# First projection in two token halves, one block's statistics on ScalarE, a shorter root, and where weight work is placed

## The chip, the cores and the metric

The kernel runs on one core of one Trainium2 chip. The metric is device microseconds (us) of one execution; before the change three runs gave 808.19, 809.09 and 808.35 us, median 808.35. Engines are called PE (TensorE, matmuls), PEld (its weight loads), DVE (VectorE), ACT (ScalarE), POOL (GpSimd) and SP (SyncE, which here issues nearly all DMAs). Each engine runs its own list of instructions strictly in the order of the list.

## What is computed

Layer norm of `x` (2048 tokens of 512), then a sliding-window attention with 32 heads of 16 and a window of 256, and beside it a SwiGLU block of width 1792; the output is `x + attention * silu(swiglu)`.

```
xn = _layernorm(x)                                   # (x - mean) / sqrt(var + 1e-5), no affine
qkv = (xn @ wqkv) -> q, k, v                         # 32 heads of 16
scores = q . k * 16**-0.5, masked to 0 <= i - j < 256
s = softmax(scores) @ v, heads joined, @ wo
h = silu(xn @ w1) * (xn @ w3)                        # 512 -> 1792
g = silu(h @ w2)                                     # 1792 -> 512
out = x + s * g
```

## The kernel before

**Precision.** Each operand of a dense matmul is cut into two 16-bit parts, a high and a low one, and a product is made as three matmuls: high·high, low weight·high token, high weight·low token. Weights are first scaled by a power of two that comes from the sum of squares of the rows. So a weight block passes through these steps: a DMA load in f32; its squares summed (`squares`, on ACT at L249 or on DVE at L251); the sums cast to bf16 (`cast`, L261, DVE) and summed over partitions by a one-column matmul (`powers`, L280); the scale made of them on DVE (L291, L298, L302, L304); and the cut into high and low. The cut is `split` (high on ACT, L333; low on DVE, L334) or `split_pool` (scaling and high on ACT, L342 and L343; low on POOL in four pieces, L345).

**Stages.** Tokens go in four tiles of 512 (`t` = 0 to 3). `prepare(t)` loads four blocks of 128 tokens, takes mean and variance of each (`stats`: L438 and L439, on DVE), the reciprocal root for all four at once (`rstd`), subtracts and multiplies (`centre`, L477) and turns each block on PE (`turn`, L493); ACT copies the turned block as the high part `XH` (L496), DVE makes the low part `XL` (L501). `project(t, g, k)` then makes queries (`k` = 0) or keys (`k` = 1) of eight heads (L597), stored through ACT (L614) and DVE (L618) to DRAM and fetched from there in the layout of the heads (`fetch`, L643). `value` makes the values (L567). In the steady part each of 32 units (`t`, `g`, `p`) runs a first pass for the row maxima (`pass1`, scores at L667, maxima on DVE at L681) for a later unit, and a second pass (`pass2`: scores at L748, mask added on DVE at L755, exponential on ACT at L758, values at L776), with pieces of the SwiGLU between them (`gate_up`, L1048, tanh on ACT at L1063, products on DVE at L1067 and L1072, a copy at L1081; `down`, L1273). The weights of the SwiGLU are loaded and prepared during the first tile (`measure`, `measure_down`): `measure` handles two blocks of `w1` and `w3`, four squares of 512 columns.

**The order of the work.** PE's list is the order in which the program is written. The lists of DVE, ACT, POOL and SP are set by a planner at build time; `urgent()` raises an instruction's priority in it, and `tc.issue_after(ins)` keeps the instructions inside from being planned before `ins`. That is a matter of the plan alone: the order of an engine's list comes out of it, no wait on the chip. `lasts` holds such anchors: `lasts["exp"]` is the exponential issued last (L758), `behind_exp()` puts work behind it, and `lasts["emptied"]` is the DVE instruction that last freed a PSUM bank. `later(n, f)` runs `f` after `n` further pieces of PE's work.

**The start** (the part that the change rewrites). ACT fills `KA[1]` with ones (L1525). DVE takes the statistics of all four blocks. The root is a shift, a subtraction (L447, L448) and then a cubic and a Newton step (L451 to L459); the Newton step is kept behind the cast of the first weight sums. The centring stands behind the scale of the first weights. Matmuls of ones (`keep_busy`, L1549) fill PE while it has nothing: 24 at first, 3 ahead of the turning and 3 behind it. Then follow on PE: keys of head group 0 with the high tokens (`k00[0]`, four matmuls of 512 columns), queries likewise (`q00[0]`), the low weights of the keys (`k00[1]`), a one-column sum for the next weights (L280), the low weights of the queries (`q00[1]`), the low tokens of both, and the keys of group 1 (`k01`).

## Time and profile before

| | |
|---|---|
| median of three runs | 808.35 us |
| the profiled execution | 808.19 us, of which 806.4 us are its span (first to last instruction) and 1.79 us lie around it |
| busy, share of the span | PE 98%, DVE 78%, ACT 49%, POOL 47% |
| TensorE clock granted | full in all 40 slices |
| DMA queue of SP and ACT | 132.13 MB, 55.9% of 16 engines' span |

All times below are of that one execution, in us from the span's start. In a row of the timeline the first number is the start, the second the length, then engine, line, operation, out<-in with shapes, how many instructions are merged, and in brackets how long the engine stood idle before it and what released it. A matmul's length includes its way through the array; in a stream the next one starts long before it ends (216 ns after it for 512 columns, 109 ns for 256), so the share of busy time says little about PE, and its idle gaps a lot. In the chain of waits the profile goes back from the last instruction, at each step to what released it.

### The profile page before, as it was taken

To read this page: it belongs to the slowest core of one execution; us is meant where nothing else is said; L and a number is where in the kernel's file an instruction comes from. 1 tells how busy PE (TensorE), PEld (TensorE's weight loads), DVE (VectorE), ACT (ScalarE), POOL (GpSimd) and SP (SyncE) were. 2 spreads that over 40 slices of the span, in tenths; PEclk is the share of its full clock that TensorE was granted. 3 is DMA by queue.
4 is the path that set the end of the run, shared out by engine and by line. 5 is a ranking of instruction groups with operands and counts; after the bars stand their busy time and mean duration, and the time that the engine had idled before them with its cause. 6 is when DMAs were issued, how large, how long until landed. Compare 5 with 4: busy or idle time off the path is not lost.

```text
span 806.4 us, 23975 instructions
## 1 busy us (share of the span) xinstructions
PE 792.3 (98%) x9175; PEld 403.6 (50%) x9175; DVE 630.9 (78%) x2037; ACT 392.5 (49%) x591; POOL 377.5 (47%) x732
## 2 busy tenths in 40 slices
PE   8999999999999999999999999999999999999997
PEld 4444444444544444444445444466544754466465
DVE  8888888798898778887888888777768886875537
ACT  6878686663456535345443443434444234344411
POOL 2345357352439345355352555430346276650670
PEclk9999999999999999999999999999999999999999
DMA  9887554746666574658456733656462654334431
GB/s 282 241 259 241 176 177 121 260 121 196 189 194 197 151 241 129 220 150 268 118 180 177 216 110 94 187 150 186 133 169 84 160 135 132 87 89 158 129 93 59
DMA packets 109859, 134.19 MB, mean 166 GB/s; under 512 B 18928, under 2 KB 64944, under 8 KB 109744
## 3 DMA queue, kind: packets, MB, share of 16 engines
q1 hardware_dynamic: 109456, 132.13, 55.9%
q8 instruction: 72, 1.18, 0.6%
q10 hardware_dynamic: 288, 0.52, 0.2%
q14 instruction: 43, 0.35, 0.1%
HBM read 91.23 MB, written 36.57 MB: 158 GB/s over the span
## 4 chain that ended last, share of the span: by engine, by line
PE 83%; DVE 6%; ACT 6%; DMA 2%; issue 2%; SPq 1%; POOL 0%; DVEq 0%; ACTq 0%
PE m L1048 30%; PE po L776 9%; PE m L1273 9%; PE m L597 8%; PE m L1191 8%; PE s L748 5%; PE m L1325 4%; PE m L567 4%; PE s L667 3%; PE po L667 2%; ACT pt L758 1%; DVE junk L681 1%; ACT slot L342 1%; DMA slot<-in_B_w_dram 1%; ACT slot L343 1%
## 5 line engine op out<-in xcount | busy, mean ns | idle before, releaser
L1048 PE MATMUL m<-XH,slot 128*128 128x512 f16 x896 | 267.3, 380 | 1.3 <-DVE slot L618 0.8
L758 ACT ACTIVATE pt<-s,es 128x1024 f32<-128x1024 f32 x152 | 167.6, 1113 | 190.9 <-DVE s L755 179.2
L1048 PEld LDWEIGHTS <-slot 128*128 128x128 f16 x1344 | 124.9, 98 | 155.2 <-issue 11.5
L1048 PE MATMUL m<-XL,slot 128*128 128x512 f16 x448 | 169.8, 379 | 0.0
L755 DVE TENSOR_TENSOR s<-s,MK 128x256 f32<-128x256 f32 (+2 forms) x280 | 118.8, 435 | 51.9 <-PE s L748 48.9
L681 DVE CUSTOM_DVE_ANT_0 junk<-s,MW 128x320 bf16<-128x320 f32 x276 | 134.1, 486 | 17.6 <-PE s L667 9.8
L339 POOL TENSOR_TENSOR slot<-slot,slot 128x256 f16<-128x256 f32 (+1 forms) x86 | 57.6, 692 | 126.8 <-ACT slot L1081 56.7
L345 POOL TENSOR_TENSOR slot<-slot,slot 128x128 f16<-128x128 f32 x168 | 68.8, 445 | 69.7 <-ACT slot L343 67.7
L681 DVE CUSTOM_DVE_ANT_0 junk<-po,MW 128x320 bf16<-128x320 f32 x172 | 83.5, 485 | 4.7 <-DVE al L298 0.4
L1273 PE MATMUL m<-slot,slot 128*128 128x512 f16 x336 | 78.6, 380 | 0.1
L776 PE MATMUL po<-pt,V 64*32 64x320 f32 (+4 forms) x2880 | 77.2, 342 | 1.5 <-DVE pp L304 1.5
L597 PE MATMUL m<-XH,slot 128*128 128x512 f16 x240 | 70.9, 380 | 1.1 <-DVE slot L1067 0.7
L1191 PE MATMUL m<-slot,slot 128*128 128x256 f16 x588 | 68.4, 273 | 0.0
L1106 POOL TENSOR_TENSOR slot<-slot,slot 128x256 f16<-128x256 f32 x98 | 64.6, 672 | 1.1
L1063 ACT ACTIVATE slot<-m,sgs 128x512 f32<-128x512 f32 x56 | 38.3, 683 | 54.0 <-PE m L1048 53.8
L776 PEld LDWEIGHTS po<-pt,V 64*32 64x32 f32 x2880 | 50.4, 106 | 23.6 <-issue 2.4
L1191 PEld LDWEIGHTS <-slot 128*128 128x128 f16 x588 | 56.2, 98 | 11.4 <-issue 2.8
L1067 DVE SCALAR_TENSOR_TENSOR slot<-slot,m 128x512 f32<-128x512 f32 x56 | 38.3, 685 | 28.6 <-ACT slot L1063 27.1
L748 PE MATMUL s<-qa,KA 50*64 50x320 f16 (+3 forms) x1472 | 58.3, 259 | 0.2 <-DVE M L681 0.2
L597 PEld LDWEIGHTS <-slot 128*128 128x128 f16 x384 | 35.6, 98 | 44.6 <-issue 3.1
L748 PEld LDWEIGHTS <-KA 50*64 50x64 f16 x1472 | 30.1, 105 | 52.0 <-issue 31.4
L1273 PEld LDWEIGHTS <-slot 128*128 128x128 f16 x336 | 30.7, 98 | 38.4 <-issue 4.0
(190 smaller groups left out, 1138.8 us busy)
## 6 DMA issues: line engine op xcount, KB each, us to landing
slot<-dW SPq DMA_DIRECT2D x98, 256.0 KB
slot<-in_B_w_dram SPq DMA_DIRECT2D x56, 256.0 KB
slot<-dFold SPq DMA_DIRECT2D x48, 256.0 KB
dW<-slot SPq DMA_DIRECT2D x42, 256.0 KB
slot<-in_A_x_dram SPq DMA_DIRECT2D x30, 256.0 KB
KA<-dK SPq DMA_DIRECT2D x24, 288.0 KB
slot<-dWQ SPq DMA_DIRECT2D x24, 256.0 KB
qa<-dQ SPq DMA_DIRECT2D x30, 192.0 KB
```

What stands on the lines that cost most here:

```text
L339: op(out[:, c], a[:, c], b[:, c])
L345: nc.gpsimd.tensor_sub(lo[:, c:c + P], raw[:, c:c + P], hi[:, c:c + P])
L597: nc.tensor.matmul(cell["pp"], w[:, (a * NC + c) * P:(a * NC + c + 1) * P], b[:, c, :], start=(c, i) == parts[0][0], stop=(c, i) == parts[ ...
L681: lasts["maximum"] = nc.vector.tensor_tensor_reduce(out=junk[:, :n], in0=s[:, r, :n], in1=mask, scale=1.0, scalar=NEG, op0=ALU.add, op1=AL ...
L748: nc.tensor.matmul(s[64 * h:64 * h + 64, r, o:o + 64 * n], ka[rows, 2 * p + a, 64 * (m + 4):64 * (m + 5)], qa[rows, 2 * p + a, 64 * (m + k ...
L755: nc.vector.tensor_add(v, v, MK[:, kind, of:of + n, :].unsqueeze(1).to_broadcast([P, 2 * len(which), n, 64]))
L758: lasts["exp"] = nc.scalar.activation(pt, s, AF.Exp, scale=es)
L776: nc.tensor.matmul(cell["po"][32 * i:32 * i + 32, h, 64 * (m + k):64 * (m + k + n)], V[64 * h:64 * h + 64, (4 * t + m // 2) % VB, hd * VW: ...
L1048: nc.tensor.matmul(cell[k], w[:, (a * NC + c) * P:(a * NC + c + 1) * P], b[:, c, :], start=c == 0 and i == 0, stop=c == NC - 1 and i == 2)
L1106: nc.gpsimd.tensor_sub(lo, view, hi)
L1191: nc.tensor.matmul(cell["ps"][:, c], made[:, f:f + P], wj[:, g:g + 256], start=j == j0 and c == 0 and n == 0, stop=j == j1 - 1 and n == 2, ...
L1273: nc.tensor.matmul(ps, hh[:, a * TW + b * P:a * TW + (b + 1) * P], w[:, c * D:(c + 1) * D], start=f == f0 and i == 0, stop=f == f1 - 1 and ...
```

## The change

- `stats` of block 3 of the first tile goes to ACT: a copy with accumulation (the sum), a one-element step that makes minus the mean, a square with that as bias and accumulation (the variance); DVE only scales both sums by 1/512. For that ACT's fill of `KA[1]` goes to POOL.
- `rstd` of the first tile stays at nine operations on DVE behind `ve`. Before, each needed the one ahead of it; now two of them (both on `r0`) stand beside the chain, which is seven deep, and the hold behind the cast is gone.
- `project` can run its first part in two halves of 256 columns (tokens 0 to 255, then 256 to 511): `k00` begins with high and low weights for the first half, then for the second, then the queries. The three matmuls of ones ahead of it go.
- The squares that `measure` puts on ACT later on are planned behind `lasts["exp"]`, which is now also set by the projections' copy (L614) and by tanh (L1063). So the planner's lists for ACT, DVE, POOL and SP differ up to about 270 us of the program.

```diff
@@ squares
+        def behind(i, raw):
+            with behind_exp() if i < on_act and "emptied" in lasts else nullcontext():
+                one(i, raw)
         for i, raw in enumerate(parts):
             if apart:
-                later(apart * (i + 1), lambda i=i, raw=raw: one(i, raw))
+                later(apart * (i + 1), lambda i=i, raw=raw: behind(i, raw))
@@ prepare: stats
+            if t == 0 and b == 3:
...
+                nc.scalar.activation(junk, xts[b], AF.Copy, accum_out=acc[:, 0:1])
+                nc.scalar.activation(neg, acc[:, 0:1], AF.Copy, scale=-1.0 / D)
...
+                nc.scalar.activation(junk, xts[b], AF.Square, bias=neg, accum_out=acc[:, 1:2])
+                nc.vector.tensor_scalar(mv[:, b, :], acc, 1.0 / D, None, op0=ALU.mult)
+                return
@@ prepare: rstd
+            if t == 0:
...
+                nc.vector.tensor_scalar(r0.bitcast(I32), ve.bitcast(I32), -0.5, float(0x5F3759DF), op0=ALU.mult, op1=ALU.add)
+                nc.vector.tensor_mul(sq, r0, r0)
+                nc.vector.tensor_mul(y, sq, ve)
+                nc.vector.tensor_scalar(r0, r0, -0.5 * (9 / 64) * (3 / 8) * XS, None, op0=ALU.mult)
+                nc.vector.scalar_tensor_tensor(sq, y, -10 / 3, y, op0=ALU.add, op1=ALU.mult)
+                nc.vector.scalar_tensor_tensor(z, sq, 5.0, y, op0=ALU.add, op1=ALU.mult)
+                nc.vector.scalar_tensor_tensor(r0, sq, 5.0, r0, op0=ALU.add, op1=ALU.mult)
+                nc.vector.scalar_tensor_tensor(z, sq, 5.0, z, op0=ALU.add, op1=ALU.mult)
+                nc.vector.scalar_tensor_tensor(rs[:, b0:b1], z, -64 / 3, r0, op0=ALU.add, op1=ALU.mult)
+                return
...
-                nc.vector.scalar_tensor_tensor(r0, sq, 5.0, r0, op0=ALU.add, op1=ALU.mult)
-                with tc.issue_after(lasts["cast"].ins):
-                    nc.vector.tensor_mul(sq, r0, r0)
-                nc.vector.scalar_tensor_tensor(sq, sq, -0.5 * (3 / 8)**3 * XS, ve, op0=ALU.mult, op1=ALU.mult)
-                nc.vector.scalar_tensor_tensor(rs[:, b0:b1], sq, 1.5 * (3 / 8) * XS, r0, op0=ALU.add, op1=ALU.mult)
-                return
@@ project
+        cols = [slice(0, TW)] * len(parts)
+        if halved:
+            parts.insert(0, parts[0])
+            cols = [slice(0, TW // 2), slice(TW // 2, TW)] + cols[1:]
...
-                nc.scalar.activation(B[:, 0, :], pp, AF.Copy, scale=s)
+                lasts["exp"] = nc.scalar.activation(B[:, 0, :], pp, AF.Copy, scale=s)
@@ gate_up
-                    nc.scalar.activation(sg, cell[0], AF.Tanh, scale=sg_scale[:, f:f + 1])
+                    lasts["exp"] = nc.scalar.activation(sg, cell[0], AF.Tanh, scale=sg_scale[:, f:f + 1])
@@ the start
-    nc.scalar.activation(KA[1].rearrange("p a (b c) -> p (a b) c", c=P), onesb.unsqueeze(1).to_broadcast([P, 24, P]),
-                         AF.Copy, scale=ONE)
...
-    for a in range(4):
-        nc.gpsimd.memset(KA[2][:, a, :].bitcast(F32), TWO_ONES)
+    for ka in KA[1:]:
+        for a in range(4):
+            nc.gpsimd.memset(ka[:, a, :].bitcast(F32), TWO_ONES)
...
-    keep_busy(3, waiting[:, 0, :].rearrange("p (k q) -> p k q", q=P))
-    k00, q00 = (project(0, 0, k, ((0,), (1,), (2,)), (lambda: waiting) if k else False) for k in (1, 0))
-    run([k00[0], q00[0], k00[1]])
+    k00 = project(0, 0, 1, ((0, 1), (2,)), lambda: waiting, True)
+    q00 = project(0, 0, 0, ((0,), (1,), (2,)))
+    run(k00[:2] + q00[:2])
     qk[1][2]()
...
-    run([q00[1]])
```

How the lists stand at the three places that the prediction speaks of. Line numbers of the changed kernel run ahead of those of the kernel before: its L444, L445 and L447 are the new ACT steps, L448 DVE's scaling, L451 and L452 the statistics, L456 to L473 the root, L249 the squares, L264 the cast, L283, L294, L301 and L305 the scale, L336 and L337 the cut, L345 and L346 `split_pool`'s ACT steps, L778 the exponential, L1083 tanh, L951 the squares for `w2`.

The first place is the start on ACT and on DVE. ACT before:

```order
L1525 ACT_TABLE_LOAD
L1525 ACTIVATE KA_141<-onesb 128x3072
L249 ACTIVATE sqa,ssq<-slot_177 128x512
L249 ACTIVATE sqa,ssq<-slot_178 128x512
L333 ACTIVATE slot_307<-slot_178,sw_277 128x512
```

and with the change:

```order
L444 ACT_TABLE_LOAD
L444 ACTIVATE sqa,acc<-slot_173 128x512
L445 ACTIVATE neg<-acc 128x1
L447 ACTIVATE sqa,acc<-slot_173,neg 128x512
L249 ACTIVATE sqa,ssq<-slot_176 128x512
L249 ACTIVATE sqa,ssq<-slot_177 128x512
L336 ACTIVATE slot_317<-slot_177,sw_285 128x512
```

The two squares of the first weights (L249) now stand behind the statistics of block 3. DVE before, from the last steps of the root (`sb` is the cast of the weight sums, `rs` the root's result, `sw` the scale):

```order
L455 SCALAR_TENSOR_TENSOR r_292<-sq,r_292 128x4
L261 CAST sb<-ssq 128x2
L457 TENSOR_TENSOR sq<-r_292 128x4
L458 SCALAR_TENSOR_TENSOR sq<-sq,ve 128x4
L291 TENSOR_SCALAR al<-s 128x1
L459 SCALAR_TENSOR_TENSOR rs<-sq,r_292 128x4
L298 TENSOR_SCALAR al<-al 128x1
L302 TENSOR_SCALAR sw_277<-al 128x1
```

and with the change:

```order
L469 SCALAR_TENSOR_TENSOR sq<-y 128x4
L470 SCALAR_TENSOR_TENSOR z<-sq,y 128x4
L471 SCALAR_TENSOR_TENSOR r_300<-sq,r_300 128x4
L472 TENSOR_TENSOR z<-sq,z 128x4
L473 SCALAR_TENSOR_TENSOR rs<-z,r_300 128x4
L264 CAST sb<-ssq 128x2
L294 TENSOR_SCALAR al<-s 128x1
L301 TENSOR_SCALAR al<-al 128x1
L305 TENSOR_SCALAR sw_285<-al 128x1
```

The cast stood in the middle of the root; it now stands behind the whole of it.

The second place is SP's list at about 22 to 36 us: the stores of keys and queries of groups 0 and 1 (L621 to L625, now L641 to L645), their fetches (L643, now L663), the last projection weights (L395, now L398) and the first SwiGLU weights after them (L870, now L890). Before:

```order
L625 DMA dK_148<-slot_464 128x512
L643 DMA KA_140<-dK_147 48x2x512 x2
L643 DMA qa<-dQ_143 48x2x512 x2
L643 DMA KA_140<-dK_147 48x2x512 x2
L643 DMA qa<-dQ_143 48x2x512 x2
L624 DMA dK_148<-slot_464 128x2x512
L621 DMA dQ_144<-slot_497 128x2x512
L622 DMA dQ_144<-slot_497 128x512
L395 DMA slot_553<-in_A_wqkv_dram 128x4x128
L643 DMA KA_141<-dK_148 48x4x512 x2
L643 DMA qa<-dQ_144 48x4x512 x2
L395 DMA slot_554<-in_A_wqkv_dram 128x4x128
```

and with the change:

```order
L645 DMA dK_148<-slot_479 128x512
L644 DMA dK_148<-slot_479 128x2x512
L663 DMA KA_140<-dK_147 48x2x512 x2
L663 DMA qa<-dQ_143 48x2x512 x2
L663 DMA KA_140<-dK_147 48x2x512 x2
L663 DMA qa<-dQ_143 48x2x512 x2
L641 DMA dQ_144<-slot_512 128x2x512
L642 DMA dQ_144<-slot_512 128x512
L663 DMA KA_141<-dK_148 48x4x512 x2
L663 DMA qa<-dQ_144 48x4x512 x2
L398 DMA slot_568<-in_A_wqkv_dram 128x4x128
L398 DMA slot_569<-in_A_wqkv_dram 128x4x128
```

The first of the two weight loads moved behind the fetch of group 1, and the last store of keys ahead of the fetch of group 0.

At the head of the same stretch DVE makes the scale of the value weights (`swwv`) and stores the low part of the keys of group 1 (L618, now L638). Before:

```order
L291 TENSOR_SCALAR al<-s 128x1
L251 ISA junk,ssq<-slot_202 128x512
L251 ISA ssq 128x1
L298 TENSOR_SCALAR al<-al 128x1
L302 TENSOR_SCALAR swwv<-al 128x1
L304 TENSOR_SCALAR p2wv<-al 128x1
L618 SCALAR_TENSOR_TENSOR slot_464<-m_420,slot_464 128x512
```

and with the change:

```order
L294 TENSOR_SCALAR al<-s 128x1
L251 ISA junk,ssq<-slot_197 128x512
L251 ISA ssq 128x1
L301 TENSOR_SCALAR al<-al 128x1
L638 SCALAR_TENSOR_TENSOR slot_479<-m_435,slot_479 128x512
L305 TENSOR_SCALAR swwv<-al 128x1
L307 TENSOR_SCALAR p2wv<-al 128x1
```

The scale stood ahead of that store and now stands behind it.

The third place is ACT's list from the exponential at 108.92 us to the next one at 113.97 us. Before:

```order
L758 ACTIVATE pt_1941<-s_1928,es1_400 128x1024
L342 ACTIVATE slot28_1099<-slot28_1099,pi_1768 128x512
L931 ACTIVATE sqa_1988,ssq2_1987<-slot16_1745 128x512
L1063 ACTIVATE slot46_2003<-m1_1978,sgs_155 128x512
L343 CAST slot19_1955<-slot28_1099 128x512
L342 ACTIVATE slot8_1008<-slot8_1008,sw2_1974 128x512
L249 ACTIVATE sqa_2005,ssq_1923<-slot38_1566 128x512
L343 CAST slot24_1990<-slot8_1008 128x512
L758 ACTIVATE pt_2038<-s_2025,es1_400 128x1024
```

and with the change:

```order
L778 ACTIVATE pt_1956<-s_1943,es1_415 128x1024
L345 ACTIVATE slot28_1114<-slot28_1114,pi_1783 128x512
L249 ACTIVATE sqa_1991,ssq_1938<-slot5_1580 128x512
L1083 ACTIVATE slot46_2018<-m1_1993,sgs_155 128x512
L346 CAST slot19_1970<-slot28_1114 128x512
L249 ACTIVATE sqa_2000,ssq_1938<-slot9_1584 128x512
L345 ACTIVATE slot8_1023<-slot8_1023,sw2_1989 128x512
L951 ACTIVATE sqa_2003,ssq2_2002<-slot16_1760 128x512
L778 ACTIVATE pt_2053<-s_2040,es1_415 128x1024
```

Two squares (of slots 5 and 9) that stood ahead of the exponential at 108.92 us now stand behind it, and two other steps moved out behind the next one.

More of the change, by code (lines that the diff above doesn't have):

```diff
@@ L579, in keys, with project @@
         return KA[(t * NG + g) % 3]
-    def project(t, g, k, terms=(range(3),), scores_bank=False):
+    def project(t, g, k, terms=(range(3),), scores_bank=False, halved=False):
         cell = {}
@@ L596, in part @@
                 a, b = ((0, xh), (1, xh), (0, xl))[i]
-                nc.tensor.matmul(cell["pp"], w[:, (a * NC + c) * P:(a * NC + c + 1) * P], b[:, c, :], start=(c, i) == parts[0][0],
-                                 stop=(c, i) == parts[-1][-1])
+                nc.tensor.matmul(cell["pp"][:, cols[n]], w[:, (a * NC + c) * P:(a * NC + c + 1) * P], b[:, c, cols[n]],
+                                 start=n == 0 and (c, i) == parts[0][0], stop=(c, i) == parts[-1][-1], skip_group_check=halved)
             if n < len(parts) - 1:
```

16 lines of the change are left out of this document (9 added, 7 removed).

## Prediction

> **What bounds the kernel now.** First the page, for the busy shares.
>
> ```profile
> PE 792.3 (98%) x9175; PEld 403.6 (50%) x9175; DVE 630.9 (78%) x2037; ACT 392.5 (49%) x591; POOL 377.5 (47%) x732
> ```
>
> PE works in all but 806.4 − 792.3 = 14.1 us. Nothing is gained, then, by making another engine's work cheaper; only those 14.1 us count, and what could make them more. So next, the windows, for where they lie (PE's busy time is the first number behind the window's length):
>
> ```profile
> 0.00:13.00 13.00, 10.20 (x49) 5.09 (x50) 10.43 (x35) 8.40 (x12) 5.33 (x33) 1.00 0.92 280
> ...
> 27.00:60.00 33.00, 32.26 (x241) 14.27 (x239) 26.30 (x123) 27.51 (x61) 17.17 (x36) 1.00 0.89 256
> 60.00:100.00 40.00, 38.63 (x354) 17.67 (x353) 32.84 (x121) 29.47 (x57) 17.39 (x39) 1.00 0.67 209
> 100.00:150.00 50.00, 46.34 (x589) 23.28 (x588) 42.55 (x164) 35.95 (x67) 29.12 (x72) 1.00 0.60 176
> 150.00:250.00 100.00, 99.37 (x1167) 48.03 (x1165) 85.99 (x305) 52.40 (x75) 45.06 (x102) 1.00 0.60 186
> ```
>
> PE stands idle 2.80 us in the first 13, 0.74 between 27 and 60, 1.37 between 60 and 100, 3.66 between 100 and 150, and 0.63 in the next 100. The change moves work in the first 270 us, so some 9 us are in its reach at most. The list of PE's waits says that they are single stalls with DVE or ACT as the last to be waited for; each is shown below where it stands in the timeline, with its length and releaser in brackets, because what matters is the work ahead of the releaser.
>
> **The start, statistics to keys.** The timeline of the first 13 us:
>
> ```profile
> 6.67 0.63 ACT L249 ACTIVATE sqa<-slot 128x512 bf16<-128x512 f32 x1 [0.96 <-DMA slot<-in_A_wqkv_dram]
> ...
> 7.21 0.18 ACT L249 ACTIVATION_READ_ACCUMULATOR sqa<-slot 128x1 f32 x1
> 7.22 0.17 DVE L443 TENSOR_SCALAR ve<-mv 128x4 f32<-128x4 f32 x1
> ...
> 7.65 0.63 ACT L249 ACTIVATE sqa<-slot 128x512 bf16<-128x512 f32 x1 [0.25 <-DMA slot<-in_A_wqkv_dram]
> ...
> 8.51 0.16 DVE L261 CAST sb<-ssq 128x2 bf16<-128x2 f32 x1
> ...
> 8.72 0.19 PE L280 MATMUL s<-sb,onesb 128*128 128x1 bf16 x2 [1.03 <-DVE sb L261]
> ...
> 9.03 0.15 DVE L459 SCALAR_TENSOR_TENSOR rs<-sq,r 128x4 f32<-128x4 f32 x1
> ...
> 9.46 1.91 DVE L477 TENSOR_SCALAR slot<-slot,mv,rs 128x512 f32<-128x512 f32 x4
> 9.52 0.72 ACT L333 ACTIVATE slot<-slot,sw 128x512 f16<-128x512 f32 x1 [1.15 <-DVE sw L302]
> ...
> 10.81 1.07 ACT L496 CAST XH<-m 128x512 f16<-128x512 f32 x2 [0.57 <-PE m L493]
> ...
> 12.91 1.02 PE L597 MATMUL s<-XH,slot 128*128 128x512 f16 x4 [0.17 <-ACT XH L496]
> ```
>
> ACT's square at 6.67 and the next at 7.65 both waited for a load of 256 KB; they are 0.98 apart, so block 3, the load ahead of them, is an estimated 5.7 (and not later than 6.67). DVE has its four statistics and begins `ve` at 7.22.
>
> With the change ACT takes block 3 from 5.7: a copy with accumulation like the square (0.54 until its read of 0.18, so 0.72), the one-element step, and a square with a bias operand (0.72, as L333, and its read, 0.1 of it uncovered). The one-element step has no row. Bounds: the read of one column, 0.18, and a whole 512-column step, 0.63; I take 0.2, since it is one column. That gives 7.45, then 0.2 on DVE for the scaling: `ve` at about 7.7 instead of 7.22. The Trainium skill, "ScalarE: Activation LUTs", section "What ACT_TABLE_LOAD costs", has 186 ns plus 0.833 ns per column for a step with immediate operands, an estimated 0.19 for the one-element step, by which the sum would be the same; the rows agree on the pointer operand's further 93 ns (0.63 without, 0.72 with).
>
> The root: before, nine steps, each waiting for the one ahead, from 7.22 to 9.03, 0.2 each. Now nine again, of which two (the scaling of `r0` and its last product but one) depend on older results; such a step follows 0.1 behind (8.51 to 8.62 at the cast). 7 × 0.2 = 1.4, so `rs` begins at 9.1, as late as before: **the shorter root pays for the later statistics and no more**. But the cast of the weight sums, at 8.51 before, now stands behind the root, at 9.2. From cast to the first centring there were 9.46 − 8.51 = 0.95 (the sum on PE, three steps of the scale, their p2qk), and all of it stays: the first centring at about **10.2, 0.7 later** than now.
>
> From centring to the first keys: the copies of blocks 0 and 1 end at 10.81 + 1.07 = 11.88, now 12.6, and as the first half needs only these, `k00` can start at 12.65 instead of 12.91: 0.25 gained where 0.7 was lost. Sixteen matmuls of half the columns cost what eight whole ones do (109 and 216 ns apart). The ones that go cost nothing: they filled time in which PE waited anyway.
>
> **The start, values.** What is late next is ACT and DVE, which stay 0.7 behind. PE's list goes on through queries and low tokens to the values:
>
> ```profile
> 15.50 0.16 DVE L261 CAST sb<-ssq 128x2 bf16<-128x2 f32 x1
> ...
> 16.64 1.03 PE L597 MATMUL s<-XL,slot 128*128 128x512 f16 x4
> ...
> 21.26 0.60 ACT L614 ACTIVATE slot<-m 128x512 f16<-128x512 f32 x1 [2.10 <-PE m L597]
> ...
> 21.93 0.15 DVE L302 TENSOR_SCALAR swwv<-al 128x1 int32<-128x1 int32 x1
> ...
> 22.06 0.68 DVE L618 SCALAR_TENSOR_TENSOR slot<-m,slot 128x512 f16<-128x512 f32 x1
> ...
> 22.88 2.74 DVE L334 SCALAR_TENSOR_TENSOR wvl<-slot,swwv,wvh 128x512 f16<-128x512 f32 x4
> ...
> 23.87 0.38 PE L567 MATMUL s<-wvl,XH 128*128 128x512 f16 x1
> ```
>
> The sum for the next weights (cast at 15.50, now 16.3) stands in PE's list ahead of the low tokens, so these begin at about 16.5 instead of 16.64; the gain shrinks to 0.1. Then the scale of the value weights: `swwv` at 21.93 stood ahead of DVE's store of `k01` (L618, 22.06), and with the change it is planned behind it (the second place above). ACT's copy at 21.26 ends at 21.86, the store takes 0.68, so `swwv` comes at 22.6, 0.65 later. The four low parts stood 0.95 behind it, from 22.88, each 2.74 / 4 = 0.68 long; now they begin at 23.5 and are ready at 24.2, 24.9, 25.6 and 26.2. PE took the first at 23.87, where it had been ready at 23.6, and the others three matmuls of 0.216 apart, the last at 25.81. That one is now late by 0.4 to 0.5, and all behind it. So the start costs **+0.5**. Bounds: −0.2 (the scale in time after all, the gain of the halves cut by those 0.2 of spare) and +1.0 (block 3 at 6.2 and the one-element step at 0.63).
>
> **The loads behind it.** SP's queue, the chain of waits (start, length) and PE's stall:
>
> ```profile
> 33.34 4.63 SPq L870 DMA_DIRECT2D slot<-in_B_w_dram  x4
> ```
> ```profile
> 29.34 5.25 DMA slot<-in_A_wqkv_dram
> ```
> ```profile
> 52.72 0.69 DVE L618 SCALAR_TENSOR_TENSOR slot<-m,slot 128x512 f16<-128x512 f32 x1
> ...
> 53.46 0.59 PE L1048 MATMUL m<-XH,slot 128*128 128x512 f16 x2 [0.63 <-DVE slot L618]
> ```
>
> The chain from 24 to 55 us runs from the load at 29.34 over the DMAs, ACT's squares and copies to the store at 52.72, for which PE stands 0.63 at 53.46. The load of 29.34 moves behind the fetches of group 1, and the SwiGLU loads (33.34) stay behind it; in the window 27 to 60 the DMA engines are busy 0.89 of the time, so a load not made while PE worked at 29 is made later, an estimated 0.98 at worst; I take 0.3, as part of the DMA time to 33 was free (0.11 of this window). A delay of PE alone would vanish in the 0.63 of that stall, but the chain starts at the values, which are 0.5 late. Of 0.5 + 0.3 I count **+0.6** past 53.46 for start and loads together (bounds −0.1 and +1.4).
>
> **The squares behind exponentials.** First tile, ACT:
>
> ```profile
> 72.60 1.10 ACT L758 ACTIVATE pt<-s,es 128x1024 f32<-128x1024 f32 x1
> ```
>
> Two squares and a cut stood just ahead of it in ACT's list, where now one square for `w2` does; it comes up to 0.75 earlier. PE's idle time of 1.37 between 60 and 100 lies mostly in stalls that wait for DVE, so I take **−0.2** for them (bounds 0, and −0.45, a third of the 1.37). Then 109 to 128 us:
>
> ```profile
> 112.86 0.62 ACT L249 ACTIVATE sqa<-slot 128x512 bf16<-128x512 f32 x1
> ...
> 113.47 0.61 ACT L343 CAST slot<-slot 128x512 f16<-128x512 f32 x1
> 113.97 1.11 ACT L758 ACTIVATE pt<-s,es 128x1024 f32<-128x1024 f32 x1
> ```
> ```profile
> 112.60 0.59 PE L597 MATMUL m<-XH,slot 128*128 128x512 f16 x2 [0.73 <-DVE slot L1067]
> ...
> 115.14 0.30 PE L667 MATMUL s<-KA,qa 48*64 48x256 f16 x4 [0.74 <-ACT pt L758]
> ...
> 121.17 0.33 PE L667 MATMUL po<-KA,qa 48*64 48x320 f16 x4 [0.64 <-DVE XL L525]
> ...
> 127.70 0.70 PE L776 MATMUL po<-pt,V 64*32 64x320 f32 x9 [1.49 <-DVE pp L304]
> ```
>
> Four stalls, 0.73 + 0.74 + 0.64 + 1.49 = 3.6 us, the largest lump of all. ACT works without a break here. What counts is how many steps it has between one exponential and the next: by its list seven up to the one at 113.97 before, and seven with the change (both stand above in the part on the change); four up to the next and four with it; eleven to the one after, and eleven. Squares came in and cuts went out. A square with its read holds ACT 0.61 (112.86 to 113.47), a cast 0.5 (to 113.97): an exchange costs 0.1. So these stalls stay, **+0.1** (bounds −0.5, one step less ahead of one exponential, and +0.5, one more).
>
> **Past 150 us** only 0.63 lies idle in 100; the one tight place I find is POOL's root for the third tile:
>
> ```profile
> 184.40 1.30 POOL L339 TENSOR_TENSOR slot<-on,slot 128x256 f16<-128x256 f32 x2
> ```
> ```profile
> 188.12 0.54 DVE L477 TENSOR_SCALAR slot<-slot,mv,rs 128x512 f32<-128x512 f32 x1
> ```
>
> It stood ahead of these two products, which end at 185.70; with the change its steps lie between them and what leads to them, and three come behind the last. Such a step on four numbers a partition takes no longer than one of these products, 0.65, so the root is there by 187.7 at the latest; the centring takes it at 188.12. DVE's other work covers it: 0, and with the cover gone up to +0.6, the idle time of this window once more.
>
> The sum: 0.6 − 0.2 + 0.1 = **+0.5** on 808.19, the profiled execution, and its median lies 0.16 above that: 808.35 + 0.5 = **808.9**; from the bounds that decide (start and loads) 808.1 to 809.7.
>
> **Rivals.**
> (1) *The new plan takes the stalls of ACT away*: half to all of the 3.6 us at 112 to 128, −1.8 to −3.6, with +0.3 left of the start: 805.0 to 806.9. For it: squares that nobody waits for are now forbidden just ahead of an exponential, and ACT has no break there. Against: the equal counts.
> (2) *Slower by late loads*: from 33 us on the weights come up to 0.98 later, ACT's chain with them; then not 53.46 alone but also the stalls up to 100 us grow, four of them by 0.3 to 0.5 each: with the start's 0.5, +1.7 to +2.5, 810.1 to 810.9. It decides from the point where SP's loads land later than 33.34 + 0.5. For it: the DMA share of 0.89 and a chain whose first link is a load of 5.25. Against: the same bytes stand ahead of the SwiGLU loads in both orders.
> (3) *PE loses its clock at the start.* The first ones-matmuls have their weights loaded every 0.43 (0.15 and 0.28 of idle time), the later 17 every 3.63 / 17 = 0.214:
>
> ```profile
> 2.72 0.15 PEld L1549 LDWEIGHTS <-onesb 128*128 128x128 bf16 x1 [0.28 <-issue]
> ...
> 3.57 3.63 PEld L1549 LDWEIGHTS <-onesb 128*128 128x128 bf16 x17 [0.28 <-issue]
> ```
>
> PE waits 1.03 at 8.72; with the cast 0.7 later the first wait becomes 1.7. If a few waits in a row bring half rate back, 2.5 us of projections cost twice: +1.3 and the +0.5, 810.2. The Trainium skill, "TensorE: Matmul & The Clock Gate", "What's actually happening", wants an idle window of some 3.4 us for that, which would leave the rate as it is; its section "A second HAM failure mode: psum-queue depth-cycling" says that frequent short idling does it too. No row here shows a drop behind a wait of 1.03.
> (4) *The start does as it says* (`swwv` in time, ACT not late): −0.2 to −0.3, about 808.1.
>
> **Chances.** Forecast 0.36, (1) 0.26, (2) 0.22, (3) 0.08, (4) 0.08. A measurement of this kernel tells about 0.2%, 1.6 us, from no change: 806.7 to 810.0. Faster: 0.23 of (1). Same: 0.34 of the forecast, all of (4), 0.03 of (1), 0.02 each of (2) and (3): 0.49. Slower: 0.20 of (2), 0.06 of (3), 0.02 of the forecast: 0.28. The range goes from 805.8, which leaves about 0.11 of (1) out, to 810.7, which leaves some 0.05 of (2) out; the forecast's own is given above.
>
> **What will show it.** The first centring at 10.2 (not before 9.8, or the cast was not held up); the first half of the keys at 12.65; `swwv` at 22.6 and the second group of values at 26.7; the load behind the fetches and PE's stall near 53.5 us at 0.5 to 1.1; four stalls at 112 to 128 us that sum to 3.4 to 4.0; full spacing of 0.21 in the first projection. The prediction is wrong if those four shrink below 2.5, or if PE's idle time between 27 and 100 us, 2.1 now, changes by more than 1.

## The result, and the profile after

| | before | with the change |
|---|---|---|
| median of six runs each | 808.37 us | 813.58 us (810.29 to 814.64) |
| ratio, 95% interval | | 1.0058 (1.0048 to 1.0068) |
| the profiled execution | 808.19 us, span 806.4 | 810.29 us, span 808.5 |
| mean granted clock of the six runs | | 1.000, 0.996, 0.996, 0.995, 0.995, 0.994 |

The change made the kernel 0.58% slower, 5.2 us by the medians; 808.9 us was forecast, and the time lies outside the range. The profiled execution is the shortest of the six and the only one at full clock. (Full clock here means a mean of 0.999 or more.) So there are two parts to find: 2.1 us that its profile shows, and some 3 us that the others lose with the clock. The page, for the busy shares:

```profile
PE 792.0 (98%) x9180; PEld 403.9 (50%) x9180; DVE 631.9 (78%) x2036; ACT 391.4 (48%) x595; POOL 378.1 (47%) x736
```

PE's work is what it was; its idle time is 808.5 − 792.0 = 16.5 us instead of 14.1. The windows say where (PE's busy time behind the length):

```profile
0.00:13.00 13.00, 10.42 (x47) 5.04 (x48) 9.01 (x33) 6.48 (x14) 6.76 (x37) 1.00 0.92 278
...
27.00:60.00 33.00, 32.57 (x242) 14.45 (x241) 26.15 (x124) 27.71 (x61) 17.14 (x36) 1.00 0.86 251
60.00:100.00 40.00, 36.58 (x343) 16.60 (x344) 32.37 (x118) 30.09 (x58) 17.07 (x39) 1.00 0.68 214
100.00:150.00 50.00, 45.14 (x585) 22.68 (x584) 42.64 (x156) 34.08 (x63) 29.36 (x72) 1.00 0.52 164
150.00:250.00 100.00, 100.00 (x1173) 48.40 (x1170) 85.95 (x307) 53.19 (x79) 40.15 (x91) 1.00 0.60 186
```

Idle are 2.58 us in the start (2.80 before), 0.43 from 27 to 60 (0.74), but 3.42 from 60 to 100 (1.37) and 4.86 from 100 to 150 (3.66). In this execution the start and the loads behind it are thus not where most of the time went. PE's timeline has the stalls:

```profile
99.49 0.20 PE L288 MATMUL s<-sb,onesb 64*64 64x4 bf16 x4 [1.94 <-DVE sb L264]
...
115.78 0.30 PE L687 MATMUL s<-KA,qa 48*64 48x256 f16 x4 [0.31 <-ACT pt L778]
...
121.80 0.33 PE L687 MATMUL po<-KA,qa 48*64 48x320 f16 x4 [0.63 <-DVE XL L541]
...
129.84 1.58 PE L796 MATMUL po<-pt,V 64*32 64x320 f32 x49 [2.99 <-DVE pp L307]
```

Of the four stalls before, at 112.60, 115.14, 121.17 and 127.70, the first is gone, the second 0.31 instead of 0.74, the third as it was; the last has doubled from 1.49 to 2.99, and there is a new one of 1.94 at 99.49. Set against the kernel before, matmul by matmul, PE is 0.24 us late at the stall near 53.5, 0.49 at 66, 0.47 at 75.4, 2.6 at 99.5, 0.64 at 115.8 (the new stall is given back, most of it where the two shrank), 2.14 at 129.84, 3.2 at 149 (another wait for a sum, 0.92, given back as well by 237), and 2.1 at the end. **In the profiled execution most of the loss that stays is the doubled stall**, 1.5 of 2.1 us.

What makes it, first on DVE and then on POOL:

```profile
126.73 2.04 DVE L301 TENSOR_SCALAR al<-al 128x4 int32<-128x4 int32 x1
128.68 0.68 DVE L1092 SCALAR_TENSOR_TENSOR slot<-m,slot 128x512 f32<-128x512 f32 x1
129.28 0.41 DVE L541 TENSOR_TENSOR XL<-po,XH 128x256 f16<-128x256 f32 x1
```
```profile
124.08 4.66 POOL L348 TENSOR_TENSOR slot<-slot,slot 128x128 f16<-128x128 f32 x12
```

A shift of four numbers per partition on DVE (L301, 0.16 us in the median) lasts 2.04, to 128.77; POOL's twelve subtractions run without a break to 128.74. Behind the shift wait the product L1092 and the low part L541, and for these PE. (The row names `pp` as the releaser; the low part ended at 129.69, about 0.15 us ahead of PE's start.) In the kernel before:

```profile
126.19 0.45 DVE L298 TENSOR_SCALAR al<-al 128x4 int32<-128x4 int32 x1
```
```profile
123.48 3.13 POOL L345 TENSOR_TENSOR slot<-slot,slot 128x128 f16<-128x128 f32 x8
```

The same shift took 0.45, to 126.64, and POOL's run of eight ended at 126.61. In both, DVE's step ends when POOL stops. POOL's run is longer because ACT made another cast (L346) at 126.07, right behind the exponential, where before it made two squares: the change moved squares out of that place and a cut into it. A longer run alone does not make the long wait, though: the same kernel, run again, shows that next.

### The profile page after: what moved, and what is told of

The parts are those of the page before. It is cut to its first block, busy times and chain, and to the rows that moved or that the text cites. A ratio compares the mean times of both kernels' runs of the same rounds, so it can differ in the third digit from the quotient of the medians.

```text
span 808.5 us, 23984 instructions
## 1 busy us (share of the span) xinstructions
PE 792.0 (98%) x9180; PEld 403.9 (50%) x9180; DVE 631.9 (78%) x2036; ACT 391.4 (48%) x595; POOL 378.1 (47%) x736
## 4 chain that ended last, share of the span: by engine, by line
PE 83%; DVE 6%; ACT 5%; issue 2%; DMA 2%; POOL 1%; SPq 0%; ACTq 0%; DVEq 0%; POOLq 0%
PE m L1068 30%; PE po L796 9%; PE m L1293 9%; PE m L617 8%; PE m L1211 8%; PE s L768 5%; PE m L583 4%; PE m L1345 4%; PE s L687 3%; PE po L687 2%; DMA slot<-in_B_w_dram 1%; ACT slot L345 1%; DVE junk L701 1%; ACT pt L778 1%; ACT slot L346 1%
## 5 line engine op out<-in xcount | busy, mean ns | idle before, releaser
L778 ACT ACTIVATE pt<-s,es 128x1024 f32<-128x1024 f32 x152 | 167.6, 1113 | 189.4 <-DVE s L775 182.0
L1083 ACT ACTIVATE slot<-m,sgs 128x512 f32<-128x512 f32 x56 | 38.3, 684 | 55.5 <-PE m L1068 54.6
```

What stands on the lines that cost most here:

```text
L778: lasts["exp"] = nc.scalar.activation(pt, s, AF.Exp, scale=es)
```

## Experiments

Each run stands beside runs of the kernel before on the same chip (medians 808.41 to 808.74).

**The changed kernel again**, for an execution below full clock.

> The changed kernel once more, for a profile of an execution of the longer kind (five of its six gave 812.9 to 814.6 us with a mean granted clock of 0.995, the profiled one 810.29 with 1.00). Theory 1: the clock is lost behind the longest stall of PE, 2.99 us before 129.84 us. Then a slice of the page near 130 us shows the granted clock below full, some 3 to 4 us of time are lost there and the rest of the program is as in the first profile. Rival: the clock is lost in the start, where PE waits 0.98 and 0.56 us; then the first slice shows it.

811.8 us at a clock of 0.998. The windows of the start (the number before the last two is the granted clock):

```profile
11.00:12.00 1.00, 0.94 (x7) 0.93 (x8) 1.00 (x3) 0.41 (x2) 0.00 (x0) 0.77 1.11 330
12.00:13.00 1.00, 1.00 (x6) 1.00 (x5) 1.00 (x3) 0.70 (x2) 0.00 (x0) 0.50 1.18 248
13.00:14.00 1.00, 1.00 (x7) 1.00 (x6) 1.00 (x2) 0.73 (x2) 0.00 (x0) 0.50 1.15 270
14.00:15.00 1.00, 1.00 (x7) 0.69 (x6) 0.14 (x1) 0.73 (x3) 0.00 (x0) 0.52 1.15 307
```

The clock is at half for some 3.4 us in the first projection, behind waits of 1.46 and 0.56 us: this time the rival. The sum of (1 − clock) over these windows is 1.7 us, a clock of 1 − 1.7 / 810 = 0.998. So the theory met with its opposite in the start. The stall near 130 us was 1.46, not 2.99, and the one at 101.64, 1.95 long, cost no clock. DVE's shift, then POOL's run beside it:

```profile
128.88 0.51 DVE L301 TENSOR_SCALAR al<-al 128x4 int32<-128x4 int32 x1
```
```profile
126.24 4.67 POOL L348 TENSOR_TENSOR slot<-slot,slot 128x128 f16<-128x128 f32 x12
```

The lists are the same, and POOL runs its twelve subtractions without a break, to 130.91. But here the shift came free at 129.39, when the one subtraction beside it ended, and not with the run. It was 1.53 us shorter, and so was PE's stall: the two executions of one kernel show that **the held shift is worth the whole doubling of the stall**. They also show that the length of POOL's run only allows the long wait and doesn't decide it.

**The start alone, and the plan alone.**

```diff
@@ e1_start_only, from the changed kernel
-            with behind_exp() if i < on_act and "emptied" in lasts else nullcontext():
-                one(i, raw)
+            one(i, raw)
-                lasts["exp"] = nc.scalar.activation(B[:, 0, :], pp, AF.Copy, scale=s)
+                nc.scalar.activation(B[:, 0, :], pp, AF.Copy, scale=s)
-                    lasts["exp"] = nc.scalar.activation(sg, cell[0], AF.Tanh, scale=sg_scale[:, f:f + 1])
+                    nc.scalar.activation(sg, cell[0], AF.Tanh, scale=sg_scale[:, f:f + 1])
@@ e2_plan_only, from the kernel before: the same lines put in
```

> The changed start alone (statistics of block 3 on ScalarE, root, halves, memsets on POOL); squares, projection copy and tangent planned as before. Theory 1 (the plan of the squares costs the time): 808.0 to 808.9 us, stalls at 112 to 128 us as before the change (0.7, 0.7, 0.6, 1.5), clock full in all runs. Rival (the start costs it, its 0.5 us delay of the values carried on): 810 us or more, with the long stall near 129 us.

> The kernel before with the new anchors for the squares alone. Theory 1: 810 to 814.5 us, with a stall of about 1.9 us near 99 us (PE at a sum, waiting for the cast), one of about 3 us near 129 us, and runs with a clock of 0.995. Rival (the start): 808 to 808.7, as before.

The start alone: 809.85 us, ratio 1.0015 (1.0004 to 1.0027); six of twelve runs at full clock, 809.05 to 809.51, the others up to 814.1. That is above the 808.0 to 808.9 of theory 1, whose full clock in all runs failed too; nor is it the rival, as the stall near 129 stayed at 1.49. The plan alone: 811.39, ratio 1.0033 (1.0018 to 1.0047), 809.07 to 814.3, with stalls of 1.95 us at 99.01 and 2.99 at 130.81. Both parts cost, by the medians the plan more. e1's own profile fell on a run of 814.1 us and holds the strongest case of DVE kept waiting:

```profile
244.22 4.80 DVE L710 TENSOR_SCALAR NM<-M 128x16 f16<-128x16 f32 x1
```
```profile
244.56 1.60 POOL L345 TENSOR_TENSOR slot<-slot,slot 128x128 f16<-128x128 f32 x4
246.08 0.41 POOL L1035 CAST slot<-slot 128x256 f16<-128x256 f32 x1
246.44 1.59 POOL L345 TENSOR_TENSOR slot<-slot,slot 128x128 f16<-128x128 f32 x4
247.98 0.68 POOL L1036 TENSOR_TENSOR slot<-slot,slot 128x256 f16<-128x256 f32 x1
248.59 0.41 POOL L1035 CAST slot<-slot 128x256 f16<-128x256 f32 x1
249.08 0.67 POOL L1036 TENSOR_TENSOR slot<-slot,slot 128x256 f16<-128x256 f32 x1
```

A conversion of 16 columns takes 4.80 us, to 249.02. POOL's four, one, four, one and one instructions follow each other from 244.56 to 249.00; its next begins at 249.08. In the kernel before the same step took 0.42. Behind it PE stood 2.54 us at 250.83, and the clock was at half for 3.4 us from 251.37 on. This kernel has the squares planned as before the change, so a long wait of DVE does not need the new plan.

**The scale from PSUM**, in the changed kernel (e3) and in the one before (e4).

```diff
+        psum = s is not None and n == 4 and inv is not None
...
+                    at = s[:, 1, WIN:WIN + n] if psum else al
-                    nc.vector.scalar_tensor_tensor(al, s[:, 1, WIN:WIN + n], 2.08, al, op0=ALU.mult, op1=ALU.add)
+                    nc.vector.scalar_tensor_tensor(at, s[:, 1, WIN:WIN + n], 2.08, al, op0=ALU.mult, op1=ALU.add)
+                    if psum:
+                        made(at)
         def chain():
+            if not psum:
+                made(al)
+        def made(al):
             nc.vector.tensor_scalar(al.bitcast(I32), al.bitcast(I32), 24, 23, op0=ALU.logical_shift_right,
                                     op1=ALU.logical_shift_left)
```

The edit does two things at once. The shift and the two products behind it read PSUM, and they are made at once, urgently, where they stood behind two further pieces of PE's work.

> The changed kernel, with the scale of the SwiGLU weights worked out on DVE from PSUM instead of from SBUF (the sum is left in the bank and the shift and the two products read it there). Theory 2: DVE's shift at 126.73 us took 2.04 instead of 0.17 us because POOL, which ran twelve subtractions without a break until 128.74, kept it from SBUF; with an operand in PSUM it isn't held. Then no such step lasts over 0.3 us, the stall of 2.99 us falls to 1.5 or less, the clock stays full and the time is 808.3 to 809.5 us. Rival: the stall is made by ACT's cuts or the product behind it; then it stays above 2.5 us and the time at 812 to 814.

> The kernel before, with the scale of the SwiGLU weights worked out from PSUM as in e3. Theory 2 (DVE's small steps on SBUF wait for POOL's unbroken runs, before the change too): the shift at 126.19 us (0.45 us, until POOL's run of eight ended at 126.6) is not held, the stall of 1.49 us at 127.70 falls to about 0.6 as in e3, and the time to 807.2 to 807.9 us. Rival (the stall belongs to ACT's copy and the product behind it): 1.3 us or more of the stall stay, and the time within 0.3 us of the kernel before.

e3: 809.41 us, ratio 1.0012 (1.0001 to 1.0022), and 808.08 to 808.55 in the three runs at full clock; the stall near 129 us is 0.65, and the shift isn't held (another step, with its source in SBUF, still lasts 0.92). The stall near 99 us is gone as well, since the planner put the two squares ahead of the exponential again. The full clock that was expected failed: nine of twelve ran below it, the profiled one in the start, behind a wait of 1.83. e4: **807.45 us, ratio 0.9989 (0.9980 to 0.9998)**; the stall of 1.49 is 0.74. DVE, then POOL, of e4:

```profile
125.31 0.17 DVE L306 TENSOR_SCALAR s<-s 128x4 int32<-128x4 int32 x1
...
125.72 0.15 DVE L310 TENSOR_SCALAR pi<-s 128x4 int32<-128x4 int32 x1
125.79 0.15 DVE L312 TENSOR_SCALAR pp<-s 128x4 f32<-128x4 f32 x1
125.86 0.41 DVE L533 TENSOR_TENSOR XL<-po,XH 128x256 f16<-128x256 f32 x1
126.19 0.68 DVE L1080 SCALAR_TENSOR_TENSOR slot<-m,slot 128x512 f32<-128x512 f32 x1
```
```profile
122.94 3.13 POOL L353 TENSOR_TENSOR slot<-slot,slot 128x128 f16<-128x128 f32 x8
```

The shift and the two products run at 0.15 to 0.17 in the midst of POOL's run (to 126.07). That much of theory 2 holds in both: with their source in PSUM the steps are not held. But the time gained is not theirs alone. The low part `XL`, for which PE waits, now stands ahead of the product (L1080), where before it stood behind it (L1072, 0.68 us long); of the 0.75 that the stall lost in e4, the held shift can explain 0.28 (0.45 less 0.17). And PE was 0.51 ahead at 97.45 already. So e4 prices the edit as a whole, and the rival's product isn't ruled out as a part of the stall.

**More ones at the start** (`keep_busy(24)` becomes `keep_busy(29)`).

> The changed kernel with 29 matmuls of ones at the start instead of 24. Theory 3: in part of its executions PE has run out of ones so early that it waits 1.5 to 1.8 us for the cast, and the granted clock is then 0.5 for 3.4 us from about 11.5 us on (1.4 to 1.6 us lost, as in the run 'again'). Five more ones (1.08 us) keep the wait under 0.9 us: no execution loses clock in the start, the fastest stay at 810.2 or above, the median falls by up to 1 us to 812.5 to 813.5, since the stalls near 99 and 129 us stay and may still cost clock. Rival (the clock is lost at those two stalls alone): the median stays at 813.5 and a start at half rate is still seen.

813.71 us, ratio 1.0054 (1.0041 to 1.0067): the rival, as for the median. The wait in the start is gone, and the profile shows where the clock goes otherwise:

```profile
101.00:102.00 1.00, 1.00 (x5) 0.35 (x3) 0.93 (x7) 0.86 (x3) 0.39 (x1) 0.67 0.87 263
102.00:103.00 1.00, 1.00 (x4) 0.39 (x3) 1.00 (x11) 0.00 (x0) 0.00 (x0) 0.50 1.06 404
103.00:104.00 1.00, 1.00 (x4) 0.37 (x3) 0.12 (x2) 0.00 (x0) 0.75 (x4) 0.50 1.03 377
104.00:105.00 1.00, 1.00 (x4) 0.40 (x3) 0.00 (x0) 0.56 (x1) 0.69 (x4) 0.63 0.99 381
...
131.00:132.00 1.00, 0.19 (x8) 0.21 (x16) 0.96 (x7) 0.63 (x2) 0.00 (x0) 1.00 0.43 72
132.00:133.00 1.00, 1.00 (x28) 0.71 (x20) 0.96 (x7) 0.97 (x2) 0.94 (x2) 0.53 0.28 72
133.00:134.00 1.00, 1.00 (x40) 0.79 (x32) 0.78 (x4) 0.26 (x1) 1.00 (x3) 0.50 0.62 180
134.00:135.00 1.00, 1.00 (x31) 0.45 (x15) 0.00 (x0) 0.00 (x0) 1.00 (x4) 0.50 0.01 4
135.00:136.00 1.00, 1.00 (x8) 0.35 (x5) 0.68 (x1) 0.00 (x0) 1.00 (x2) 0.77 0.00 0
```

Behind the stall of 1.96 at 99.89 and behind that of 2.99 at 131.81 the clock is at half for 3.4 us, and each time the sum of (1 − clock) is 1.7 us. This execution's span is 812.2, 3.7 more than that of the profiled one with the same stalls at full clock: 3.4 for the clock, 0.4 at the stall near 54 us. Two such losses give a mean clock of 1 − 3.4 / 812 = 0.996; the runs of the changed kernel below full clock have 0.994 to 0.996, which leaves room for a third in some.

**Statistics back on DVE** (the branch for block 3 taken out of e1).

> The changed start with block 3's statistics back on DVE (shorter root, halves, memsets on POOL kept), squares planned as before. My theory of the start (ScalarE's statistics, 0.5 us later, hold up the root, with it the cast and all behind): the cast at about 8.9 us and the first centring at about 9.8 instead of 10.36, the second group of values at 26.3 to 26.6 instead of 26.79, and 0.3 to 0.6 us less than e1_start_only in executions at full clock: 808.5 to 809.0. Rival (the statistics are not it; the order behind them is): the centring earlier but the values at 26.8 and the time as in e1.

808.42 us, ratio 0.9999 (0.9991 to 1.0008), 808.18 at the least against 809.05: 0.9 less than e1, and a little less than expected. The cast is at 8.64, the first centring at 9.61, the second group of values at 26.05. The statistics on ScalarE were thus what the start lost; one of eleven runs was below full clock instead of six of twelve.

**One pair of blocks' squares not held back.**

```diff
-            with behind_exp() if i < on_act and "emptied" in lasts else nullcontext():
+            with behind_exp() if held and i < on_act and "emptied" in lasts else nullcontext():
...
-        sb = squares([raws[0][0], raws[1][0], raws[0][1], raws[1][1]], on_act=4 if f > 2 else 2, apart=apart)
+        sb = squares([raws[0][0], raws[1][0], raws[0][1], raws[1][1]], on_act=4 if f > 2 else 2, apart=apart, held=f != 8)
```

> The changed kernel, with the squares of one pair of weight blocks (8 and 9) planned as before the change and not behind an exponential. Their sum is what PE waits for at 99.49 us. Theory 1 (squares held back make a sum late for which PE is already waiting): that stall of 1.94 us is gone, though most of its time comes back as stalls near 112 to 116 us as before the change, so executions at full clock gain 0 to 0.5 us (809.8 to 810.3); the stall at 129.84 stays; the clock is lost there alone, and the median falls by about 1.6 us, to 811.5 to 812.5. Rival (another cause holds up the sum, or the clock is lost at 129 us alone): the stall near 99 us stays above 1 us, or the median stays at 813.5.

The stall near 99 us is gone (the 0.20 left there waits for another step), those of 112 to 116 us are back (0.72 and 0.83), the shortest run is 809.95: as expected. The median, 812.79 of six runs from 809.95 to 816.82, is above what was expected, and clocks of 0.993 to 0.998 remain; with so wide a spread it says little. In its profile the clock is at half for 3.4 us behind the stall of 2.99, at 131.39.

**The plan without the held step, and the best of all.** e12 is e2 with the scale from PSUM, e10 is e8 with it.

> The kernel before, with the new anchors for the squares (as e2) and the scale worked out from PSUM (as e4). Theory 2 (the plan costs time chiefly where it lengthens POOL's run under DVE's small steps): no step of DVE is held for 2 us, no stall above 1 us near 128 us, 807.1 to 808.0 us at full clock, within 0.5 us of e4_before_psum. Rival (the new places of the squares and cuts cost time by themselves): 809 us or more at full clock.

> What the runs so far make the best: the changed start with block 3's statistics on DVE (e8), squares planned as before, the scale worked out from PSUM (e4). If the two add, 807.0 to 807.6 us, 0.9 to 1.4 us less than before the change; if the start's new order gives back what the scale gains, 808.0 or more.

e12: 807.35 us, ratio 0.9983 (0.9974 to 0.9992), all eleven runs at full clock, 0.1 us less than e4 by the medians. ACT's list from 108.76 to 126 us is that of the changed kernel, cut behind the exponential included, and POOL's run there is sixteen subtractions long, yet the stall near 127 is 0.65. **From 109 to 128 us the new places of the squares and cuts cost nothing by themselves.** For the place near 99 us e12 says nothing: its two squares stand ahead of the exponential, as before the change. e10: 807.09 us, ratio 0.9981 (0.9973 to 0.9990), all at full clock: faster than both kernels.

**Stalls made on purpose**, in e10: DVE makes four (e13) or two (e14) copies for nobody.

```diff
+                    for _ in range(extra):
+                        nc.vector.tensor_scalar(ppool.tile([P, D], BF16, name="junk", bufs=1)[:, 0:WIN], s[:, 0, 0:WIN], 1.0, None, op0=ALU.mult)
```

> e10_best with a stall put in on purpose: behind the scale of weight blocks 8 and 9 DVE makes four copies of 256 or 320 columns that nobody uses (0.4 to 0.5 us each), before it goes on with the maxima for which PE waits. Theory 3 (a stall of PE of some 2 us or more costs the clock for 3.4 us in most executions, 1.6 us on top of the stall itself): one new stall of 1.3 to 2.2 us near 100 us; executions at full clock up to 1.5 us above e10_best, 807.5 to 808.6 us, and some at 0.998 with 1.5 us more. Rival (the clock goes by something else in the changed kernel, not by the stalls): all executions at full clock, as with e10_best.

> The same with two such copies: a new stall of 0.5 to 1.2 us. Theory 3: no longer than the stalls that the kernel before has, so no clock lost; 807.1 to 807.8 us and all executions at full clock. Rival: as many executions below full clock as in e13.

e13: 810.37 us; the stall is 2.54 at 103.42. Four of nine runs have a clock of 0.998, and in one of them the windows show it:

```profile
103.00:104.00 1.00, 0.58 (x15) 0.33 (x23) 0.99 (x7) 0.50 (x2) 0.77 (x3) 0.50 1.06 399
104.00:105.00 1.00, 1.00 (x37) 0.72 (x29) 0.72 (x5) 0.00 (x0) 0.24 (x2) 0.50 1.04 399
105.00:106.00 1.00, 1.00 (x36) 0.61 (x28) 0.00 (x0) 0.00 (x0) 0.74 (x4) 0.50 0.74 275
106.00:107.00 1.00, 1.00 (x26) 0.40 (x11) 0.00 (x0) 0.00 (x0) 0.67 (x5) 0.80 0.02 8
```

e14: 810.07 us; stalls of 0.88 and, not intended, 1.52 at 109.89 and 1.16 at 123.10. Ten of eleven runs at 0.999 or above, one at 0.996. The longer stall thus takes the clock in about half the executions and the shorter ones hardly ever. Both expected times were missed, by about 2 us: the copies kept more waiting than reckoned. And in e13 the runs at 0.998 (810.28 to 810.44) are no longer than the others (810.17 to 810.7): there what came behind the stall hid the loss, which it did not in e6.

**When a stall takes the clock.** The profiles answer this together. In each of them, while PE has work, all changes of the granted clock lie whole multiples of 3.413 us apart, so they stand on a grid: in e2 the clock is at half from 99.58 to 102.99 and from 130.30 to 133.71, and 30.72 = 9 × 3.413. What counts is PE's idle time between two points of that grid, summed. It was 1.95 and 2.47 ahead of the two drops in e2, 1.95 and 2.99 in e6, 2.95 in e11, 2.10 in e13, 2.67 in e1, and in the start 2.02 in 'again' and 2.10 in e3. In no stretch of the fourteen profiles without a drop behind it was it more than 1.71 (the start of e11). In the profile of the changed kernel a point of the grid fell into each long stall: of the 1.94 us 1.68 lie in one stretch, and the 2.99 us are cut into 1.68 and 1.31. So it was luck that this execution kept its clock.

## Why the prediction was wrong

**What bounds the kernel, and the start: right, its price a little low.** The first centring came at 10.36 (10.2 forecast), the first keys at 12.84 (12.65), `swwv` at 22.64 (22.6), the second group of values at 26.79 (26.7). The start's price, put at +0.5, is 0.9 by e1's shortest run (809.05, against 808.11 of the kernel before beside it) and by what e8 takes away again; by PE's place in the two profiles it is 0.50 and 0.43 at the values, and past 164 us 0.75 in e1. The lines of the changed kernel, DVE and PE:

```profile
10.36 1.91 DVE L493 TENSOR_SCALAR slot<-slot,mv,rs 128x512 f32<-128x512 f32 x4
...
22.64 0.14 DVE L305 TENSOR_SCALAR swwv<-al 128x1 int32<-128x1 int32 x1
```
```profile
26.79 0.38 PE L583 MATMUL m<-wvh,XH 128*128 128x512 f16 x1
```
```profile
53.70 0.59 PE L1068 MATMUL m<-XH,slot 128*128 128x512 f16 x2 [0.32 <-ACT slot L345]
```

**The loads: too high.** PE's stall near 53.5 is 0.32, not 0.5 to 1.1, and start and loads together cost 0.24 there and 0.49 at 66 us instead of 0.6; in two of the later profiles the stall was 1.04 and 1.07, so the price varies between executions.

**The squares at 72.60: wrong in sign, small.** The exponential came a little earlier (72.45), but the stall behind it went from 0.84 to 1.23, still waiting for DVE's maxima: 0.2 more instead of 0.2 less.

**The squares behind exponentials: here the prediction failed.** Its two terms for them add up to −0.1; from 66 to 129.8 us PE lost 1.65 (0.49 late, then 2.14). For 60 to 100 us it put −0.2 on PE's idle time, which grew by 2.05. (PE's idle time from 27 to 100 us, one of its own signs of being wrong, went from 2.1 to 3.9.) For 109 to 128 us it said that what counts is how many steps ACT has between one exponential and the next; seven, four and eleven, as before, so that "these stalls stay". The counts were right and the wrong thing to count. The four stalls do sum to 3.9 us, inside the 3.4 to 4.0 that were to show it, but by luck: the first two shrank by 1.2 and the last grew by 1.5. Two things went past the counts. First, a square has a reader: the sum that PE makes of it. Held behind the exponential at 95.39, two squares were made at 96.88 and 97.63 instead of 93.70 and 94.46; they were done at 98.36, their cast stood in DVE's list behind a product and a mask and ran at 99.30, and PE stood 1.94 us at the sum. The stall is gone in e11, e3 and e12, where the squares stand ahead of the exponential:

```profile
95.39 1.11 ACT L778 ACTIVATE pt<-s,es 128x1024 f32<-128x1024 f32 x1
...
96.88 0.63 ACT L249 ACTIVATE sqa<-slot 128x512 bf16<-128x512 f32 x1
...
97.63 0.63 ACT L249 ACTIVATE sqa<-slot 128x512 bf16<-128x512 f32 x1
```
```profile
93.70 0.64 ACT L249 ACTIVATE sqa<-slot 128x512 bf16<-128x512 f32 x1
...
94.46 0.63 ACT L249 ACTIVATE sqa<-slot 128x512 bf16<-128x512 f32 x1
...
95.09 1.09 ACT L758 ACTIVATE pt<-s,es 128x1024 f32<-128x1024 f32 x1
```

(ACT after, then before.) The two stalls at 112 to 116 did not shrink as rival (1) had it. They shrank because PE came there late: with the stall near 99 us gone they are back (0.72 and 0.83 in e11, 0.73 and 0.82 in e12). Second, and dearer in this profile, which step it was that filled a place: a cast behind the exponential feeds POOL, and POOL's longer run can hold DVE longer. That a shift of 0.45 us, which takes 0.17 where POOL is idle, stood ahead of the stall at 127.70 could be read in the trace of before; the forecast took the stall as ACT's and quoted PE's row alone. 1.5 us more came from this stall; it is gone where the shift came free early ('again') and where it reads PSUM (e3 and e12).

**The clock: right as a mechanism, with the wrong chance, place and number.** The sum had no term for it. Rival (3), given 0.08, had +1.3 for 2.5 us at half rate in the start. It happens there in part of the runs (the profiles of 'again' and e3), and behind the new stalls (e2, e6 and e11), 1.7 us each time. Five of the six runs were below full clock; they have no profile, so where each lost it is not known. 2.1 us of the profile's own and the 3.4 of e6's clock make 5.5, about the 5.2 of the medians. Idle stretches of 1.95 to 2.99 us were enough, though not in every execution. The Trainium skill, "TensorE: Matmul & The Clock Gate", "What's actually happening", wants an idle window of some 3.4 us; by that none of these would have cost clock, and the runs do not agree.

**Open.** Why DVE's shift came free after one subtraction in one execution and only at the end of POOL's run in four others with the same plan (the first profile, e2, e6 and e11) isn't settled. Nor is the exact idle time that costs the clock, between 1.71 and 1.95 us in one stretch. What made single runs of 816.8 us in e11 and 817.3 us in e14 wasn't seen in a profile.

## What to carry to other kernels

When work is moved off an engine's urgent steps, follow it to its readers on both sides: the one that already waits for its result, and the one that the work in its old place now feeds. Look in the trace for short steps that last far longer than others of their kind, and for what ended when they ended; here three tiny steps, read from PSUM instead of from SBUF and made sooner, were worth 1 us in the kernel before. And price a stall with what it may do to the clock: in e6 two stalls of 2 and 3 us cost 3.4 us more than themselves.

## What the runs showed of the hardware

- A step of DVE from SBUF to SBUF (shifts and conversions of 4 or 16 columns) was held while POOL ran, and ended within 0.05 us after the end of one of POOL's instructions. Mostly that was the first or the second end: the shift took 0.51 us in 'again', another step 0.92 in e12, and POOL's run went on. But in four profiles the shift waited for the rest of a run of twelve (2.04 us), and in e1 a conversion through eleven instructions (4.80 us). With a source in PSUM the shift took 0.17 us beside POOL in all six kernels that have it (e3, e4, e10, e12, e13, e14). The Trainium skill, "SBUF — State Buffer", "Who interferes with whom", has the port pair that the two share and says that the loser waits for the whole instruction; the short waits agree with that, and the waits of 2.04 and 4.80 us were longer than one instruction.
- The granted clock fell to 0.50 for 3.4 us, or 3.413 by the grid, where PE's idle time between two points of the grid came to 1.95 us or more, and never where it was 1.71 or less. The stalls behind which it fell were of 1.95, 1.96, 2.54 and 2.99 us, and in the start of 1.46 and 0.56 or 1.83 and 0.57. Outside the start no stall of up to 1.52 us was followed by it in a profile.
